# Layer 2's gate and value products over two units at once, 16-bit sums for norms, two raw loads from ScalarE, and a new table of shifts

## The chip, the cores and the metric

The kernel runs on one core of one Trainium2 chip. The metric is the device time of one execution in microseconds. A difference is told by the median of several runs.

## What is computed

Attention over 4 batches and 8 heads keeps, for each of 576 queries, the 32 largest scores. Its output, 2304 rows of 512, goes through two gated layers with an inner width of 1536. The weights arrive as 64-bit numbers, which the kernel converts itself; all other inputs have 32 bits.

```python
scores = scale * np.matmul(q, k.transpose(0, 1, 3, 2))
kth = np.partition(scores, -top_k, axis=-1)[..., -top_k:-top_k + 1]
scores = np.where(scores >= kth, scores, -1000000000.0)
attn = np.exp(scores - np.max(scores, axis=-1, keepdims=True))
attn = attn / (np.sum(attn, axis=-1, keepdims=True) + 1e-09)
x = np.matmul(attn, v)
...
xn = x / np.sqrt(np.mean(x * x, axis=-1, keepdims=True) + 1e-06) * rms_g
g = xn @ w_gate
x = (g / (1.0 + np.exp(-g)) * (xn @ w_val)) @ w_out
...
gate = 1.0 / (1.0 + np.exp(-(x @ w_gate2)))
out = (gate * (x @ w_val2)) @ w_out2
```

## The kernel before

**Units and tiles.** The 2304 rows form 18 units of 128 rows: four full ones for each batch of inputs, and one for each two batches that holds the 64 rows left over of both. For a unit, attention works through eight score tiles `sp` of 128 x 576 (144 in all). `attend` (line 721) makes one: TensorE writes the scores, VectorE finds the 32 largest by four MAX8 and three MATCH_REPLACE8, ScalarE takes the exponential `e`, VectorE masks it, ScalarE and GpSimd split it in two 16-bit parts `ph`, a DMA transposes them, and TensorE multiplies with v into `pv`. Two score banks rotate, so a score product waits until VectorE is done with the tile two before it.

**Precision.** Each 32-bit operand of a product is held as two 16-bit parts, and each product is three: high with high, high with low, low with high. `product` (line 862) writes 128 x 512 results from 48 such products (four blocks `m` of 128, four blocks of the contraction, three pairs), with the weights as the stationary operand and 128 columns of the unit's transposed rows moving. `out2` (line 1000) has the unit stationary and 512 columns of weights moving.

**Layers.** Layer 1 of a unit is `enter1` (norm and transpose), `gate1` for each of three slices `j` (products `pg` and `pw`, then tanh, scale and products on ScalarE and GpSimd, result `ht1`), and `out1` (product `py`, result `yt` in two 16-bit parts). Layer 2 is `gate2` for each slice (`pg` and `pw` from `yt`, result `ht2`) and `out2` (`po`). `gated` (line 884) holds what gate1 and gate2 share. Layer 1's weights stay in SBUF; those of layer 2, converted once and parked in DRAM, are read again for each batch by `load2` (line 980) into the seven buffers that raw weights use too. `BATCHES` (line 59) groups the units for layer 2: one, then eight pairs, then one. The two units of a pair share the loads, but each has its own products, its own scale `gsc` and its own `yt`.

**Sums for norms.** `scale_of` (line 680) and `out1` add a column over all partitions by a 32-bit product with `ones32`; `prep_piece` (line 500) spreads a column over the partitions by a 32-bit product `wmt` with the unit matrix.

**Raw weights.** `load_f32` (line 465) fetches a 128 x 512 block of 64-bit numbers. The first seven (`FIRST`) are issued by ScalarE, all others by SP. For layer 1's weights a block takes two VectorE instructions (`dec` and the joining one), one on ScalarE and one on GpSimd.

**The order.** Nothing is issued as it is written. `Scheduler.record` collects every operation with a priority, and `order` (line 260) simulates the engines with the costs of `cost` (line 224): it always takes the operation that can begin first, and among those the smallest priority. `SHIFTS` (line 64) adds a number, a tenth of it in microseconds, to the priority of each group of operations. `SLACK` says by how much an operation of TensorE counts as late after its producer (1 us, or 2.5 after SP's) when the scheduler looks for operations that are safe to take. The outcome is one fixed order for each engine and for the queue of SP; an instruction that must wait holds all behind it on its engine. Every row of the profile therefore carries the line that issues them, 385.

Of the kernel before, what the change touches and what calls it, by code (L numbers as in the profile page):

```python
# [46 lines left out]
SLACK = (1000.0, 2500.0)  # L47
# [13 lines left out]
FIRST = 7  # L61
# [82 lines left out]
class _Op:  # L144
    __slots__ = "eng calls cost lat prio deps users waits tiles start end idx new later base safe".split()
# [10 lines left out]
class Scheduler:  # L156
# [67 lines left out]
    def cost(self, eng, method, args, kw, writes, reads):  # L224
# [6 lines left out]
        if eng == "tensor":  # L231
            rate = 0.6 if method == "matmul" and kw["rhs"].shadow.dtype == F32 else 2.4
            return math.prod(out.shape[1:]) / rate + 2.7, 200
# [7 lines left out]
        if eng == "scalar":  # L241
            if method == "dma_start":
                return self.move(method, out, n)
            return n * 0.8333 + (51 if psum else 93) + 93 * (ptrs + ("accum_out" in kw)), 200
        if eng == "gpsimd":
            if method == "tensor_tensor":
                return (516 if n == 1 else n * (1.88 if mybir.dt.size(out.dtype) == 2 else 2.1) + 149), 100
# [12 lines left out]
    def order(self):  # L260
# [3 lines left out]
        for op in self.ops:  # L264
            op.users, op.waits, op.start, op.end, op.new, op.later, op.safe = [], len(op.deps), 0.0, None, [], [], 0.0
# [35 lines left out]
        def choose(reach):  # L301
            best = None
            for eng in self.ENGINES:
                pick = None
                for op in ready[eng]:
# [10 lines left out]
                    key = (max(0.0, max(at, op.safe if eng == "tensor" else 0.0) - now[eng] - PATIENCE), op.prio, op.idx)  # L316
# [7 lines left out]
        while len(out) < len(self.ops):  # L324
# [40 lines left out]
            for u in op.users:  # L365
                late = SLACK[op.eng == "sync"] if u.eng == "tensor" else 0.0
                u.start = max(u.start, op.end + OWN if u.eng == op.eng != "sync" and not op.calls[0][0].startswith("dma") else done)
                u.safe = max(u.safe, done + late)
# [20 lines left out]
def topk_attention_moe_kernel(  # L389
# [33 lines left out]
    ones32 = const.tile([P, P], F32, name="ones32")  # L423
# [715 lines left out]
```

## Time and profile before

| what | value |
| --- | --- |
| median of 3 runs | 1242.55 us (1242.1 to 1243.56) |
| the profiled execution, its own time | 1239.67 us |
| its span, first to last instruction | 1237.6 us |
| TensorE busy | 1120.6 us, 17020 products |
| VectorE busy | 994.3 us |
| ScalarE busy | 857.3 us |
| GpSimd busy | 844.0 us |

The profile is of one execution. A busy time is the union of an engine's instructions. Products overlap in the pipeline, so the length of one product's record says less than the distance from one start to the next, or than a block's share of the chain of work that ended last. An idle time of an engine is put down to the event that ended it. PE is TensorE, PEld its weight loads, DVE VectorE, ACT ScalarE, POOL GpSimd and SP the queue of SyncE.

### The profile page before, as it was taken

The page shows a single profiled execution, that of the slowest core. Times are in us where ns is not written, and L with a number is a line of the kernel's source. Part 1 is how long each engine was busy: PE and PEld are TensorE (multiplying, and loading weights), DVE is VectorE, ACT ScalarE, POOL GpSimd, SP SyncE. Part 2 cuts the span into 40 slices and gives each one's busy share as a digit, 9 for nine tenths or more (in the row PEclk, how much of TensorE's full clock was granted, in tenths as well). Part 3 has the DMA queues.
Part 4 walks back from the last instruction along what each step waited for, and adds up shares of the span by engine and source line. Part 5 has one row for each costly group of instructions (what it writes and reads, how often), then busy time and mean ns, then how long its engine had stood idle before and what let it go on. Part 6 is the DMA issues. An engine that isn't in the chain of part 4 may idle for free.

```text
span 1237.6 us, 41694 instructions
## 1 busy us (share of the span) xinstructions
PE 1120.6 (91%) x17020; PEld 963.3 (78%) x17020; DVE 994.3 (80%) x2571; ACT 857.3 (69%) x1536; POOL 844.0 (68%) x966
## 2 busy tenths in 40 slices
PE   2776374689998999999999999999999999999998
PEld 1433263689798789978996999699789969997976
DVE  5899999898796999999889899998759999970001
ACT  5999889887686577686966577578657666762522
POOL 5898899897676568685876667587657666762430
PEclk9989576699999999999999999999999999999999
DMA  9895797889968765779868586868766766854347
GB/s 281 280 264 157 238 265 221 205 258 235 211 152 187 180 147 137 137 178 189 187 144 192 115 191 136 210 132 191 179 114 139 181 153 122 193 121 136 138 122 262
DMA packets 323775, 225.27 MB, mean 182 GB/s; under 512 B 278400, under 2 KB 286592, under 8 KB 323584
## 3 DMA queue, kind: packets, MB, share of 16 engines
q1 hardware_dynamic: 322576, 218.95, 72.7%
q10 hardware_dynamic: 1008, 3.67, 0.8%
q8 instruction: 133, 2.18, 0.7%
q14 instruction: 58, 0.48, 0.1%
HBM read 147.06 MB, written 14.16 MB: 130 GB/s over the span
## 4 chain that ended last, share of the span: by engine, by line
PE 60%; DVE 15%; ACT 8%; DMA 5%; issue 5%; POOL 5%; SPq 1%; ACTq 0%; POOLq 0%; DVEq 0%
PE pg L385 17%; PE pw L385 16%; PE py L385 9%; PE po L385 9%; DVE m L385 5%; DVE w L385 5%; PE sp L385 4%; PE pv L385 3%; DVE e L385 2%; DMA kr<-in_k_dram 1%; POOL ph L385 1%; PE wlo L385 1%; ACT raw L385 1%; ACT e L385 1%; DMA pt<-ph 1%
## 5 line engine op out<-in xcount | busy, mean ns | idle before, releaser
L385 DVE MAX8 m<-w 128x8 f32<-128x576 f32 x432 | 314.5, 749 | 1.5
L385 PEld LDWEIGHTS <-wl 128*128 128x128 f16 x5184 | 293.1, 98 | 1.7 <-issue 0.7
L385 POOL TENSOR_TENSOR ph<-e,ph 128x64 f16<-128x64 f32 (+1 forms) x288 | 204.3, 733 | 79.3 <-ACT ph L385 76.9
L385 DVE MATCH_REPLACE8 w<-m,w 128x576 f32<-128x576 f32 x288 | 213.0, 743 | 0.0
L385 PEld LDWEIGHTS <-w1v 128*128 128x128 f16 (+1 forms) x2640 | 150.3, 98 | 24.1 <-POOL w1v L385 16.8
L385 POOL TENSOR_TENSOR sg<-sg,sv 128x512 f32<-128x512 f32 x105 | 133.7, 1274 | 48.0 <-ACT sv L385 45.1
L385 ACT ACTIVATE e<-sp,nb,sc 128x576 f32<-128x576 f32 x144 | 116.1, 827 | 66.6 <-POOL nb L385 47.2
L385 PE MATMUL pg<-xt,w1g 128*128 128x128 f16 x2592 | 154.4, 220 | 2.9 <-DVE ym L385 1.3
L385 PE MATMUL pg<-yt,wl 128*128 128x128 f16 x2592 | 155.4, 220 | 0.7 <-DVE p2t L385 0.7
L385 PEld LDWEIGHTS <-w1o 128*128 128x128 f16 (+1 forms) x2640 | 152.9, 100 | 3.8 <-issue 2.6
L385 POOL TENSOR_TENSOR ht<-sg,ht 128x512 f16<-128x512 f32 x105 | 121.7, 1160 | 47.7 <-ACT ht L385 45.3
L385 PE MATMUL pw<-xt,w1v 128*128 128x128 f16 x2592 | 153.5, 219 | 0.7 <-ACT sf L385 0.6
L385 PE MATMUL pw<-yt,wl 128*128 128x128 f16 x2592 | 153.6, 219 | 0.0
L385 PEld LDWEIGHTS <-w1g 128*128 128x128 f16 (+1 forms) x2624 | 149.7, 98 | 3.6 <-issue 3.1
L385 PE MATMUL py<-ht,w1o 128*128 128x128 f16 x2592 | 150.2, 221 | 0.5 <-POOL ht L385 0.5
L385 PE MATMUL po<-wl,ht 128*128 128x512 f16 x648 | 144.4, 379 | 0.0
L385 ACT ACTIVATE ph<-e 128x576 f16<-128x576 f32 x144 | 96.3, 677 | 64.9 <-DVE e L385 56.9
L385 DVE MAX8 m<-sp 128x8 f32<-128x576 f32 x144 | 106.9, 757 | 35.8 <-PE sp L385 33.3
L385 PE MATMUL sp<-kt,qt 128*128 128x512 f16 (+3 forms) x640 | 94.1, 298 | 37.0 <-DVE e L385 25.1
L385 DVE SCALAR_TENSOR_TENSOR e<-sp,m,e 128x576 f32<-128x576 f32 x144 | 115.1, 809 | 3.2 <-ACT e L385 1.2
L385 PEld LDWEIGHTS <-ht 128*128 128x128 f16 x648 | 61.7, 98 | 70.0
L385 PEld LDWEIGHTS <-qt 128*128 128x128 f16 (+1 forms) x640 | 49.1, 103 | 80.2 <-DVE e L385 18.8
(167 smaller groups left out, 1849.8 us busy)
## 6 DMA issues: line engine op xcount, KB each, us to landing
wl<-w2g SPq DMA_DIRECT2D x60, 512.0 KB, 4.8
wl<-w2v SPq DMA_DIRECT2D x60, 512.0 KB, 4.8
wl<-w2o SPq DMA_DIRECT2D x60, 512.0 KB, 5.2
raw<-in_moe_w_out_dram SPq DMA_DIRECT2D x24, 512.0 KB, 5.1
raw<-in_moe_w_val_dram SPq DMA_DIRECT2D x21, 512.0 KB, 5.2
raw<-in_moe_w_gate_dram SPq DMA_DIRECT2D x20, 512.0 KB, 4.5
qr<-in_q_dram SPq DMA_DIRECT2D x32, 128.0 KB, 3.5
kr<-in_k_dram SPq DMA_DIRECT2D x16, 256.0 KB, 3.5
```

The source lines that it names most:

```text
L385: getattr(eng, method)(*map(real, a), **{n: real(x) for n, x in k.items()})
```

## The change

`gate2` runs over a pair. `product` takes the number of blocks `M` itself; for a pair it is 2, and each product moves 256 columns, the two units side by side, so that one call makes half of a slice for both units. `out1` writes its result into a `yt` that holds both units of a batch, two of which rotate (`YT`). In `gated` layer 2's tanh is taken unit by unit, since each has its own scale. `out2` finds its operands in the new layout. The first and the last batch keep one unit and 128 columns.

The sums for norms and `wmt` become one 16-bit pass: `top` reads the upper half of each 32-bit number as bfloat16, of the column and of the unit matrix; `ones` is bfloat16.

`FIRST` goes from 7 to 2. `cost` gets other numbers for products, for raw blocks and for their sums. The slack behind a producer now delays an operation of TensorE in the simulation itself, and only from 250 us on; the choice of safe operations is gone. `SHIFTS` is new throughout: entries from -259 to 382 before, from -1796 to 2230 now.

```diff
 OWN = 130.0
-SLACK = (1000.0, 2500.0)
+SLACK = (1000.0, 2500.0, 250000.0)
...
 AHEAD = 8
-FIRST = 7
+FIRST = 2
+YT = 2
...
 SHIFTS = (
...
 )
...
             rate = 0.6 if method == "matmul" and kw["rhs"].shadow.dtype == F32 else 2.4
-            return math.prod(out.shape[1:]) / rate + 2.7, 200
+            return max(math.prod(out.shape[1:]) / rate + 2.5, 28 if out.shape[-1] > 1 else 200 if rate < 1 else 60), 200
         if eng == "vector":
...
                 return self.move(method, out, n)
-            return n * 0.8333 + (51 if psum else 93) + 93 * (ptrs + ("accum_out" in kw)), 200
+            words = any(x.tile.args[2].startswith("raw") for x in reads)
+            return n * 0.8333 + (51 if psum else 93) + (75 if words and psum else 35 if words else 0) + 93 * (ptrs + ("accum_out" in kw)), 200
         if eng == "gpsimd":
             if method == "tensor_tensor":
+                if any(x.tile.args[2].startswith("raw") for x in reads):
+                    return n * 2.1 + 180, 100
                 return (516 if n == 1 else n * (1.88 if mybir.dt.size(out.dtype) == 2 else 2.1) + 149), 100
...
                             at = max(at, dma - BACKLOG)
-                    key = (max(0.0, max(at, op.safe if eng == "tensor" else 0.0) - now[eng] - PATIENCE), op.prio, op.idx)
+                    key = (max(0.0, at - now[eng] - PATIENCE), op.prio, op.idx)
                     if pick is None or key < pick[0]:
...
             for u in op.users:
-                late = SLACK[op.eng == "sync"] if u.eng == "tensor" else 0.0
-                u.start = max(u.start, op.end + OWN if u.eng == op.eng != "sync" and not op.calls[0][0].startswith("dma") else done)
-                u.safe = max(u.safe, done + late)
+                late = SLACK[op.eng == "sync"] if u.eng == "tensor" and op.end > SLACK[2] else 0.0
+                u.start = max(u.start, op.end + OWN if u.eng == op.eng != "sync" and not op.calls[0][0].startswith("dma") else done + late)
             for u in op.users + op.later:
...
     const = pool("const", 1)
-    ones32 = const.tile([P, P], F32, name="ones32")
-    nc.vector.memset(ones32, 1.0)
+    ones = const.tile([P, P], BF16, name="ones")
+    nc.vector.memset(ones, 1.0)
     mhalf = const.tile([P, 1], F32, name="mhalf")
...
+    def top(x):
+
+        return x.bitcast(BF16).rearrange("p (f a) -> p f a", a=2)[:, :, 1]
+
     def pow2_scale(m, n, name, pl=None, out=None):
...
         t = ps_m.tile([P, P], F32, name="wmt", tag="mm", lane="wps")
-        nc.tensor.matmul(t, lhsT=m.to_broadcast([P, P]), rhs=eye, start=True, stop=True)
+        nc.tensor.matmul(t, lhsT=top(m).to_broadcast([P, P]), rhs=top(eye), start=True, stop=True)
         m = tiny.tile([P, 1], F32, name="wx")
...
         t = ps_m.tile([P, 1], F32, name="kvt", tag="mm", lane="kvt")
-        nc.tensor.matmul(t, lhsT=ones32, rhs=n, start=True, stop=True)
+        nc.tensor.matmul(t, lhsT=ones, rhs=top(n), start=True, stop=True)
         return pow2_scale(t, 1, "kv", out=(sc[0][:, p, a : a + 1], sc[1][:, p, a : a + 1]))
...
-    def product(ps, b, k, ws, rhss):
-
-        M = spread(b)[0]
+    def product(ps, M, k, ws, rhss):
+
         with E.group():
...
-    def gated(b, k, rhs, wg, wv, gsc, vsc, silu, name, bufs, last=False, behind=None, sq=None):
-
-
-
-        M, U = spread(b)
+    def gated(mu, k, rhs, wg, wv, gsc, vsc, silu, name, bufs, last=False, behind=None, sq=None):
+
+
+
+        M, U = mu
         pg = ps_m.tile([P, M, U, P], F32, name="pg", tag="mm", lane=name)
...
             E.after(behind)
-        product(pg, b, k, [wg], [rhs])
-        pg = flat(pg)
+        product(pg, M, k, [wg], [rhs])
         sg = mo.tile([P, 512], F32, name="sg", bufs=3, lane=name)
-        nc.scalar.activation(sg, pg, AF.Tanh, scale=gsc)
+        if silu:
+            pg = flat(pg)
+            nc.scalar.activation(sg, pg, AF.Tanh, scale=gsc)
+        else:
+            for x, a in enumerate(gsc):
+                nc.scalar.activation(sg.rearrange("p (m u r) -> p m u r", m=M, u=U)[:, :, x], pg[:, :, x], AF.Tanh, scale=a)
         ht = htp.tile([P, 2, M, U, P], F16, name=name, bufs=bufs)
...
             pw = pw()
-            product(pw, b, k, [wv], [rhs])
+            product(pw, M, k, [wv], [rhs])
             nc.vector.scalar_tensor_tensor(out=sg, in0=sg, scalar=1.0, in1=flat(pw), op0=ALU.add, op1=ALU.mult)
...
         pw = pw()
-        product(pw, b, k, [wv], [rhs])
+        product(pw, M, k, [wv], [rhs])
         sv = m1.tile([P, 512], F32, name="sv", tag="tmp", bufs=3, lane="sv" + name)
...
             t = ps_m.tile([P, 1], F32, name="yn", tag="mm", lane="yn")
-            nc.tensor.matmul(t, lhsT=ones32, rhs=n, start=True, stop=True)
+            nc.tensor.matmul(t, lhsT=ones, rhs=top(n), start=True, stop=True)
             m = tiny.tile([P, 1], F32, name="ym")
...
             ys[b] = pow2_scale(m, 1, "y")
-            yts[b] = []
         s, i = ys[b]
...
         product(
-            py, b, k, [lay1["o"][0][j] for j in range(NJ)],
+            py, M, k, [lay1["o"][0][j] for j in range(NJ)],
             [columns(b, [ht1[b, j, x] for x in range(U)]) for j in range(NJ)],
...
         nc.scalar.activation(f, flat(py), AF.Copy, scale=s)
-        yt = mo.tile([P, 2, M, U, P], F16, name="yt", bufs=2)
-        hi, lo = (flat(yt[:, a]) for a in range(2))
+        d, x = inside[b]
+        if x == 0:
+            yts[d] = mo.tile([P, 2, CPJ, 2, P], F16, name="yt", bufs=YT)
+            in2[d] = []
+        f = f.rearrange("p (c r) -> p c r", r=P)
+        hi, lo = (yts[d][:, a, :, x] for a in range(2))
         nc.scalar.activation(hi, f, AF.Copy)
         nc.gpsimd.tensor_tensor(out=lo, in0=f, in1=hi, op=ALU.subtract)
-        yts[b].append(yt)
-        if k < U - 1:
-            return
         a = tmul(i, ik, name="ya")
...
             nc.vector.tensor_scalar(gsc[:, j], lay2["g"][2][:, j].bitcast(F32), a, 0.5, op0=ALU.mult, op1=ALU.mult)
-        in2[b] = (columns(b, yts[b]), gsc, a)
+        in2[d].append((gsc, a))
...
-    def gate2(d, b, j, k):
+    def gate2(d, j, k):
         for n in "gv":
...
                 load2(d, n, j)
-        rhs, gsc, _ = in2[b]
+        U = len(batches[d])
+        rhs = lambda c, a: yts[d][:, a, c, 0:U]
         last = d == len(batches) - 1
-        ht2[b, j, k] = gated(
-            b, k, rhs, w2[d, "g", j], w2[d, "v", j], gsc[:, j : j + 1], state["c2"][0][:, j : j + 1], False, "ht2", 6, last,
+        ht2[d, j, k] = gated(
+            (CPJ // U, U), k, rhs, w2[d, "g", j], w2[d, "v", j], [g[:, j : j + 1] for g, _ in in2[d]], state["c2"][0][:, j : j + 1], False, "ht2", 6, last,
             state["c2"][0] if d == 0 else None
...
             w = w2[d, "o", j]
-            for b in batches[d]:
-                ht = columns(b, [ht2[b, j, k] for k in range(len(groups[b]))])
-                for x, u in enumerate(groups[b]):
+            U = len(batches[d])
+            ht = lambda c, a: ht2[d, j, c * U // CPJ][:, a, c % (CPJ // U)]
+            for x, b in enumerate(batches[d]):
+                for u in groups[b]:
                     if j == 0:
...
                                 n += 1
-        for b in batches[d]:
+        for x, b in enumerate(batches[d]):
             for u in groups[b]:
-                osc = tmul(in2[b][2], state["c2"][1], name="osc")
+                osc = tmul(in2[d][x][1], state["c2"][1], name="osc")
                 o = mo.tile([P, 512], F32, name="acc", tag="sg", bufs=3, lane="acc")
...
             groups.append([next(units) for _ in range(n)])
+    inside = {b: (d, x) for d, bs in enumerate(batches) for x, b in enumerate(bs)}
     halves = lambda b: range(len(groups[b]))
...
     ]
-    second = lambda d: [(5.4, gate2, (d, b, j, k)) for j in range(NJ) for b in batches[d] for k in halves(b)] + [
+    second = lambda d: [(5.4, gate2, (d, j, k)) for j in range(NJ) for k in range(len(batches[d]))] + [
         (7.8 * sum(len(groups[b]) for b in batches[d]), out2, (d,))
...
```

The new order shows first on ScalarE at the very start of the program. `raw` is a block of raw weights, `gr` the squared gain, `qr`, `kr` and `vr` are the first q, k and v, `kvn` their sums of squares. Before:

```order
L385 DMA raw_109<-in_moe_w_gate_dram 128x1024
L385 DMA raw_118<-in_moe_w_gate_dram 128x1024
L385 DMA raw_124<-in_moe_w_gate_dram 128x1024
L385 DMA raw_128<-in_moe_w_gate_dram 128x1024
L385 DMA raw_132<-in_moe_w_val_dram 128x1024
L385 DMA raw_134<-in_moe_w_val_dram 128x1024
L385 DMA raw_136<-in_moe_w_val_dram 128x1024
L385 ACT_TABLE_LOAD
L385 ACTIVATE raw_109<-raw_109 128x512
L385 ACTIVATE raw_118<-raw_118 128x512
L385 ACTIVATE gr_120<-gr_120 128x512
L385 ACTIVATE raw_124<-raw_124 128x512
```

And with the change:

```order
L392 DMA raw_109<-in_moe_w_gate_dram 128x1024
L392 DMA raw_118<-in_moe_w_gate_dram 128x1024
L392 ACT_TABLE_LOAD
L392 ACTIVATE raw_109<-raw_109 128x512
L392 ACTIVATE raw_118<-raw_118 128x512
L392 ACTIVATE gr_120<-gr_120 128x512
L392 ACTIVATE qn_77_148,qn_147<-qr_124 128x256
L392 ACTIVATE ks_161,kvn_162<-kr_126 128x576
L392 ACTIVATE qn_77_148<-qr_124,qs_159 128x4x2x64
L392 ACTIVATE vt_177,kvn_178<-vr_130 128x640
L392 ACTIVATE qr_124<-qr_124,qs_159 128x256
L392 ACTIVATE ks_161<-kr_126,kvs_180 128x9x64
```

Five issues are gone from the front, the table load stands behind two, and the squares of q, k and v stand ahead of all later raw blocks.

On VectorE, the last rows ahead of the first MAX of a score tile (`wps` and `wmt` are sums over a piece of weights). Before, with the rows of the second and third piece in front of it:

```order
L385 TENSOR_SCALAR dec_356<-raw_280 128x512
L385 SCALAR_TENSOR_TENSOR w1v_21_355<-raw_280,dec_356 128x512
L385 TENSOR_REDUCE wx_366<-wmt_362 128x1
L385 TENSOR_SCALAR wn_373<-wx_366,g_27_153 128x1
L385 TENSOR_SCALAR p2t_377<-wn_373 128x1
L385 TENSOR_SCALAR w1vs_379<-p2t_377 128x1
L385 TENSOR_SCALAR w1vi_384<-w1vs_379 128x1
L385 MAX m_85_418<-sp_401 128x8
```

With the change:

```order
L392 TENSOR_REDUCE wm_262<-wps_230 128x1
L392 SCALAR_TENSOR_TENSOR w1g_20_256<-raw_184,dec_257 128x512
L392 TENSOR_REDUCE wx_268<-wmt_266 128x1
L392 TENSOR_SCALAR wn_273<-wx_268,g_27_152 128x1
L392 TENSOR_SCALAR p2t_276<-wn_273 128x1
L392 TENSOR_SCALAR w1gs_278<-p2t_276 128x1
L392 TENSOR_SCALAR w1gi_285<-w1gs_278 128x1
L392 MAX m_85_312<-sp_280 128x8
```

The first MAX now follows the sums of the first piece `w1g` (`wn_273`, `w1gs`) instead of those of the second (`w1vs`), behind nine blocks of raw weights instead of thirteen.

On TensorE, a `yn` that is followed by a layer 2 gate product, in the middle of the program. Before:

```order
L385 LDWEIGHTS qt_12186
L385 MATMUL sp_12496<-kt_11417,qt_12186 128x64
L385 MATMUL yn_12503<-hn_12251,ones_0_107 128x1
L385 LDWEIGHTS wl_2908_11751
L385 MATMUL pg_12505<-yt_9976,wl_2908_11751 128x128
```

With the change:

```order
L392 LDWEIGHTS w1o_25_963
L392 MATMUL py_11469<-ht_2876_11368,w1o_25_963 128x128
L392 LDWEIGHTS ones_107
L392 MATMUL yn_11674<-hn_11438,ones_107 128x1
L392 LDWEIGHTS wl_2905_11025
L392 MATMUL pg_11676<-yt_9311,wl_2905_11025 128x256
```

`yn` has a weight load of its own now, as 16-bit products do, and the product behind it makes 256 columns from one load instead of 128.

## Rows read from the trace of the kernel before

**Rows 1.** The page, part 1: busy us (share of the span) and instructions.

```profile
PE 1120.6 (91%) x17020; PEld 963.3 (78%) x17020; DVE 994.3 (80%) x2571; ACT 857.3 (69%) x1536; POOL 844.0 (68%) x966
```

**Rows 2.** Busy time by stretches: from, to, length, engines, granted clock, DMA share, GB/s.

```profile
0.00:40.00 40.00, 15.05 (x80) 9.58 (x80) 22.76 (x61) 23.22 (x45) 26.26 (x32) 1.00 0.91 286
40.00:250.00 210.00, 134.68 (x1244) 90.89 (x1243) 199.95 (x541) 190.46 (x341) 187.16 (x206) 0.74 0.83 229
...
300.00:1105.00 805.00, 796.21 (x13104) 711.43 (x13101) 716.67 (x1813) 555.57 (x1000) 548.42 (x648) 1.00 0.74 162
300.00:1237.60 937.60, 924.89 (x14911) 818.61 (x14907) 727.34 (x1846) 602.85 (x1079) 588.92 (x683) 1.00 0.71 164
```

**Rows 3.** VectorE's waits, 40 to 250 us (9 rows): total, times, longest.

```profile
DVE p2t L385 <- PE kvt L385: 1.5, 2, 1.3
...
DVE ms L385 <- ACT junk L385: 0.3, 1, 0.3
```

**Rows 4.** TensorE's waits, 300 us to the end (9 rows).

```profile
PE sp L385 <- DVE qi L385: 2.0, 1, 2.0
PE sp L385 <- DVE e L385: 1.7, 3, 1.1
...
PE kvt L385 <- ACT vt L385: 0.2, 1, 0.2
```

**Rows 5.** The chain that ended last, from 1100 us: start, us, what.

```profile
1106.94 0.42 PE pv L385 x14
...
1153.78 5.36 PE pg L385 x96
...
1196.71 12.95 PE po L385 x60
```

**Rows 6.** Groups by form, whole span: count, busy us, mean ns, idle before.

```profile
L385 PEld LDWEIGHTS <-wl 128*128 128x128 f16 x5184 | 293.1, 98 | 1.7 <-issue 0.7 <-DMA wl<-w2g 0.2
...
L385 ACT ACTIVATE sg<-pg,gsc 128x512 f32<-128x512 f32 x54 | 36.7, 679 | 15.7 <-PE pg L385 15.6
...
L385 ACT ACTIVATE qr<-qr,qs 128x256 f32<-128x256 f32 x36 | 18.1, 502 | 0.4
```

**Rows 7.** Timeline of TensorE, two places: start, us, instructions, idle before.

```profile
340.95 2.85 PE L385 MATMUL pg<-yt,wl 128*128 128x128 f16 x48
...
465.39 0.36 PE L385 MATMUL yn<-hn,ones 128*128 128x1 f32 x2
465.61 2.84 PE L385 MATMUL pw<-yt,wl 128*128 128x128 f16 x48
```

**Rows 8.** Groups by form on TensorE, 300 us to the end.

```profile
L385 PE MATMUL kvt<-kvn,ones 128*128 128x1 f32 x44 | 7.1, 242 | 1.1 <-ACT ks L385 0.9 <-ACT vt L385 0.2
L385 PE MATMUL yn<-hn,ones 128*128 128x1 f32 x32 | 5.4, 239 | 0.0
```

**Rows 9.** Timeline of all engines, 0 to 45 us.

```profile
0.72 9.31 ACTq L385 DMA_DIRECT2D raw<-in_moe_w_gate_dram  x4
...
5.34 0.69 DVE L385 SCALAR_TENSOR_TENSOR w1v<-raw,dec 128x512 int32<-128x512 int32 x1
...
10.51 1.30 ACTq L385 DMA_DIRECT2D raw<-in_moe_w_val_dram  x3
...
13.14 1.20 ACT L385 ACTIVATE raw<-raw 128x512 int32<-128x512 uint32 x2
...
20.50 0.68 ACT L385 ACTIVATE ks<-kr 128x576 bf16<-128x576 f32 x1
...
26.56 1.97 SPq L385 DMA_TRANSPOSE kt<-ks  x1
...
38.47 0.77 DVE L385 MAX8 m<-sp 128x8 f32<-128x576 f32 x1 [2.24 <-PE sp L385]
```

**Rows 10.** VectorE's waits, 0 to 40 us (6 rows, 16.6 us).

```profile
DVE g L385 <- ACT gr L385: 6.0, 1, 6.0
```

**Rows 11.** The chain that ended last, its beginning.

```profile
2.24 8.25 DMA kr<-in_k_dram
```

More of the change, by code (lines that the diff above doesn't have):

```diff
@@ L144 @@
 class _Op:
-    __slots__ = "eng calls cost lat prio deps users waits tiles start end idx new later base safe".split()
+    __slots__ = "eng calls cost lat prio deps users waits tiles start end idx new later base".split()
 class _Engine:
@@ L264, in order @@
         for op in self.ops:
-            op.users, op.waits, op.start, op.end, op.new, op.later, op.safe = [], len(op.deps), 0.0, None, [], [], 0.0
+            op.users, op.waits, op.start, op.end, op.new, op.later = [], len(op.deps), 0.0, None, [], []
         for op in self.ops:
@@ L941, in gate1 @@
         ht1[b, j, k] = gated(
-            b, k, rhs, lay1["g"][0][j], lay1["v"][0][j], gsc[:, j : j + 1], vsc[:, j : j + 1], True, "ht1", 3,
+            spread(b), k, rhs, lay1["g"][0][j], lay1["v"][0][j], gsc[:, j : j + 1], vsc[:, j : j + 1], True, "ht1", 3,
             behind=vsc if groups[b][0] < 2 else None, sq=hsq[b][:, j * U + k : j * U + k + 1],
```

32 rows, old and new, of the table SHIFTS are left out of this document.

## The prediction, made before the changed kernel was run

> **What bounds the kernel now.** I read the page first, then the table by stretches, then the waits of each stretch, and last the order of single instructions at the places the edit touches. The page says that TensorE is busy for 91% of the span and VectorE for 80% [rows 1], which settles nothing: both are means over stretches with different limits. The table by stretches tells them apart [rows 2]. Between 40 and 250 us VectorE is busy for 199.95 of 210 us, TensorE for 134.68, at a mean granted clock of 0.74 (so partly at 1.2 GHz and partly at 2.4). From 300 us to the end TensorE is busy for 924.89 of 937.6 us at a clock of 1.00 (2.4 GHz), and VectorE for 727.34. So VectorE sets the pace until about 250 us, and TensorE from 300 us on.
>
> Two further views support that. In 40 to 250 us all that VectorE waited for adds up to about 9 us, none of it longer than 1.3 us [rows 3]. From 300 us to the end the listed waits of TensorE add up to 8.6 us in 937.6 [rows 4]. From 300 us on, the end is therefore the moment at which TensorE becomes full plus the work it still has. Two things can move it: less work per product behind 300 us, or an earlier moment. What the other engines do there is hidden as long as they keep up; VectorE had 88 us to spare between 300 and 1105 us (805 less its busy 716.67) [rows 2], and ScalarE is busy for 602.85 of 937.6 us.
>
> **The wide products.** The change takes two units through layer 2's gate and value products at once, in the eight batches that have two units. Of the 5184 products of 128 columns, 4608 become 2304 of 256; the first and the last batch have one unit and stay. The chain gives the step of a product at full clock [rows 5]: 96 of 128 columns in 5.36 us are 55.8 ns each, 60 of 512 columns in 12.95 us are 215.8 ns. A straight line through the two is 0.4167 ns a column and 2.5 ns for each product, so 256 columns should take 109.2 ns where two of 128 took 111.7. That is 2.5 ns x 2304 = 5.7 us, all of it behind 300 us on the full engine. Bounds: nothing, if the step of 256 columns carries more of its own; and, if the 2.5 ns vanished wholly, 111.7 - 106.7 = 5.0 ns each, 11.5 us. I take 5.7, the value on the line.
>
> Here a page speaks for much more. The Trainium skill (TensorE: Matmul & The Clock Gate, Back-to-back issue gap) gives a sustained spacing of load and product pairs of about 81 ns at 128 columns and 131 ns at 512. An estimate from that page, in between, is 98 ns at 256, which would save 2304 x (162 - 98) = 147 us. The trace disagrees: its steps are 55.8 and 215.8 ns, in proportion to the columns. So the weight load (98 ns in its records, one per product [rows 6]) is hidden behind the moving columns already, and removing 2304 of them frees a unit that was not the limit.
>
> **The 16-bit sums.** The sums over partitions for `kvt` and `yn` are products of one column that run as two passes of 32 bits. One took 0.22 us on the full engine, from 465.39 to the next product's start at 465.61 [rows 7]. Behind 300 us there are 32 records of `yn` and 44 of `kvt` [rows 8], two to a sum, so 38 sums. What one 16-bit pass with its load will take is not in the trace. The nearest rows are 30 ns for a step of 65 columns (14 in 0.42 us) [rows 5], and those 30 ns behind a load of 98 ns in the open [rows 6], 0.13 us. I take 0.07 us, nearer the first since loads mostly run ahead, so 0.15 us x 38 = 5.7 us; the ends are 3.4 and 7.2 us. The 18 products `wmt` fall too, but they belong to the preparation of the weights, ahead of the full stretch, where TensorE has a third of its time free [rows 2]: nothing.
>
> **The start.** ScalarE now issues two loads of raw weights instead of seven. In the kernel before, the first four issues took until 10.03 us, since they waited for landed loads, the last three went out only at 10.51, and ScalarE's first useful instruction came at 13.14 [rows 9]. Behind it stood the squares of k (20.50), and with them the transposed k (issued from 26.56 to 28.53); the first MAX8 of attention began at 38.47. VectorE was busy for 22.76 of these 40 us [rows 2] and waited for 16.6, of which 6.0 for ScalarE's `gr` [rows 10].
>
> Now the table load stands directly behind two issues. The first k had landed at 10.49 us (2.24 and 8.25) [rows 11], and its squares could begin there, 10 us sooner. From the squares to the end of the transpose's issue took 8.0 us; with the transpose's landing, v's squares ahead of it and the weight sum that TensorE's order still has in front, some 5 us together, the first MAX8 comes near 24 us. VectorE's order has nine raw tiles ahead of it instead of thirteen, at two instructions each of 0.69 us [rows 9], so by 24 us VectorE has done 9 x 1.38 us and some 4 us of small operations, 16.5 us, and idled for 7 or 8 instead of 16. Not all that is won lasts, since tiles must be ready to fill the time: I take 7 us off the moment at which TensorE becomes full, with ends at 0 and 12.
>
> The five loads that ScalarE no longer issues go to SP's queue, behind k and v of the first pair and ahead of the first transposes of q and k. The three that ScalarE issued last took 1.30 us [rows 9], so five take 2.2 us and their waits for landed predecessors, inside the 10 us by which k's squares move forward.
>
> **What costs nothing.** Layer 2's tanh over 512 columns becomes two over 256 in 48 blocks, because each unit has its own scale. From 679 ns at 512 columns, and 502 ns for 256 on ScalarE [rows 6], that is 0.33 us more in each, 16 us in all on an engine that is idle for a third of the stretch [rows 2]; the bank is released 0.3 us later, and three rotate. If ScalarE's slack were gone, those 16 us would be the price. Writing `yt` for two units side by side changes strides alone. Layer 2 of a pair must now wait for the second unit's `yt`; before, the first such product stood at 340.95 us [rows 7], where TensorE was full and had other work. Two wider buffers in place of two narrow ones let out1 run further ahead. I put these two against each other at nothing, with 3 us either way.
>
> **The sum.** The profiled execution took 1239.67 us with a span of 1237.6. Less 5.7, 5.7 and 7.0, that is 1221.3. The median of the three runs, 1242.55, stands 2.9 us above the profiled execution, so I forecast **1224 us**. The terms' ends alone give 1242.55 - 11.5 - 7.2 - 12 - 3 = 1209 at best and 1242.55 - 0 - 3.4 - 0 + 3 = 1242 at worst.
>
> **Rivals.** *The start gives nothing* (chance 0.19). For it: the DMA engines are busy 0.91 of the first 40 us at 286 GB/s [rows 2]; if attention's first tiles come sooner but the raw weights do not, VectorE waits later for the same bytes. Against it: its longest wait there was for ScalarE, not for a load [rows 10]. Then 1242.55 - 11.4 = 1231 us.
>
> *TensorE waits for VectorE* (chance 0.14, slower). The whole table of shifts is new, with entries of up to 223 us where 38 was the largest, and each engine keeps its written order: a score product whose bank VectorE has not released stops everything behind it on TensorE. Before, such waits behind 300 us came to 3.7 us [rows 4]. There are about 114 score tiles left there. Priced by the order's rows, the 120th tile stands behind 769 us of TensorE work instead of 800, some 10 us more than the shorter products explain, so VectorE has to be earlier there. From 0.18 us a tile (21 us) the gain is lost and the kernel slower; at 0.35 us a tile, 40 us, the time is 1242.55 - 18.4 + 40 = 1264 us. VectorE's 88 us of idle time speak against it. Waits of 16 to 21 us, which leave no change, have 0.06.
>
> *The order fills the early gaps* (chance 0.07): TensorE is idle for 75 of the 210 us from 40 to 250 [rows 2]; if ten of these carry layer products that stood behind 300, the time is 1214, and with the other good ends near 1206.
>
> *The weight load sets the step* (chance 0.01). The steps of rows 5, which grow 3.87 times with four times the columns at one load each, speak against it. If the load and not the columns did set the 55.8 ns, half of the loads would free 2304 x 55.8 ns = 129 us, and the time would be near 1110. [...]
>
> **How the numbers follow.** My forecast has 0.53, at 1214 to 1230. Faster by more than 0.2% (2.5 us, about what a measurement can tell from no change) is the sum of forecast, lost start, filled gaps and weight loads: 0.53 + 0.19 + 0.07 + 0.01 = 0.80. Same 0.06, slower 0.14. The range 1206 to 1242 takes in the bounds and the lost start, and leaves out the slower case and the far side of the gains.
>
> **What would show it.** In the changed profile: 1152 `pg<-yt` of 256 columns, 24 of them in about 2.62 us on the chain; a `yn` step below 0.1 us; ScalarE's table load before 3 us; the first MAX8 of scores before 28 us; TensorE at 49 of 50 us from some 290 us on with listed waits under 12 us. Wrong would be a first MAX8 still beyond 35 us, waits of `sp` for VectorE above 20 us behind 300, or a block of 24 that takes much less than 2.6 us.

## The result and the profile after

The changed kernel took 1223.05 us in the median of four runs (1220.78 to 1225.63) beside 1242.32 us for the kernel before: a ratio of 0.9846, with a 95% interval of 0.9822 to 0.9869. Taken again later (last experiment) it was 1220.84 us, a ratio of 0.9808 (0.9788 to 0.9829). The forecast was 1224 us. The profiled execution took 1220.78 us with a span of 1219.0; against before's 1237.6 that is 18.6 us less, where the sum of the terms said 18.4.

The page, part 1, of the changed kernel (it answers to [rows 1]):

```profile
PE 1098.5 (90%) x14648; PEld 915.3 (75%) x14648; DVE 993.8 (82%) x2571; ACT 862.4 (71%) x1584; POOL 844.9 (69%) x966
```

Its busy time by stretches, with the columns of [rows 2]:

```profile
0.00:40.00 40.00, 14.12 (x59) 7.40 (x60) 28.83 (x80) 27.37 (x51) 26.37 (x34) 0.97 0.94 291
40.00:250.00 210.00, 129.04 (x1240) 87.10 (x1239) 199.97 (x534) 189.53 (x341) 191.37 (x209) 0.78 0.84 233
250.00:300.00 50.00, 49.09 (x877) 46.98 (x875) 46.46 (x122) 40.02 (x73) 40.94 (x47) 1.00 1.05 266
300.00:1105.00 805.00, 796.06 (x11167) 683.23 (x11164) 711.45 (x1816) 565.74 (x1053) 556.60 (x654) 1.00 0.72 163
300.00:1219.00 919.00, 906.28 (x12484) 773.78 (x12480) 718.54 (x1837) 605.45 (x1123) 586.21 (x679) 1.00 0.69 164
```

VectorE gained 6.1 us of work in the first 40 us (28.83 for 22.76) and is as full as before until 250. TensorE is full from 250 us on (49.09 of 50; 45.94 before). From 300 us to the end it is idle for 12.7 us in both kernels and busy for 18.6 us less now (906.28 for 924.89).

The start in the timeline (start, us, instructions; beside [rows 9]), and VectorE's waits of the first 40 us (total, times, longest; beside [rows 10]):

```profile
0.72 0.91 ACTq L392 DMA_DIRECT2D raw<-in_moe_w_gate_dram  x2
...
1.66 1.28 ACT L392 ACT_TABLE_LOAD   x1 [1.66 <-PEq L1142]
...
9.59 0.68 ACT L392 ACTIVATE ks<-kr 128x576 bf16<-128x576 f32 x1 [0.72 <-DMA kr<-in_k_dram]
...
16.76 3.79 SPq L392 DMA_TRANSPOSE kt<-ks  x1
...
23.82 0.77 DVE L392 MAX8 m<-sp 128x8 f32<-128x576 f32 x1 [0.65 <-PE sp L392]
```

```profile
DVE dec L392 <- DMA raw<-in_moe_w_gate_dram: 5.4, 3, 3.7
DVE p2t L392 <- PE kvt L392: 3.7, 3, 2.4
DVE ones L392 <- PEq L1142: 0.8, 1, 0.8
DVE m L392 <- PE sp L392: 0.6, 1, 0.6
```

The table load follows two issues, the squares of k wait for their own load and no longer for ScalarE, and the first MAX8 comes 14.7 us sooner. VectorE's wait for `gr` is gone; 10.5 us of waits are left of 16.6. The lead over the kernel before does not last: counted by the first MAX8 of every score tile, it is 4.0 us at the 13th tile (154.9 for 158.9) and gone at the 25th (260.0 for 257.7); by the 31st it is 8.2 us (295.4 for 303.6). VectorE is as full in both from 40 to 250 us, so what moves the tiles there is the other work that each order puts between them.

Groups by form over the whole span, of the changed kernel (count, busy us, mean ns, idle before), beside [rows 6, 8]:

```profile
L392 PE MATMUL pg<-yt,wl 128*128 128x256 f16 x1152 | 133.6, 273 | 0.0
...
L392 PE MATMUL yn<-hn,ones 128*128 128x1 bf16 x18 | 3.0, 168 | 0.0
...
L392 PEld LDWEIGHTS <-wl 128*128 128x128 f16 x2880 | 254.4, 98 | 25.6
...
L392 ACT ACTIVATE sg<-pg,gsc 128x256 f32<-128x256 f32 x96 | 41.4, 465 | 3.9 <-PE pg L392 3.1 <-PE yn L392 0.7
```

TensorE's timeline in two places with a `yn` and the product behind it, beside [rows 7]:

```profile
557.30 0.17 PE L392 MATMUL yn<-hn,ones 128*128 128x1 bf16 x1
557.32 8.20 PE L392 MATMUL py<-ht,w1o 128*128 128x128 f16 x144
...
618.42 0.17 PE L392 MATMUL yn<-hn,ones 128*128 128x1 bf16 x1
618.45 2.78 PE L392 MATMUL pg<-yt,wl 128*128 128x256 f16 x24
```

The chain that ended last holds both widths, a pair's block of layer 2 and, behind it, one of layer 1 with 128 columns, `pg` from `xt` (beside [rows 5]):

```profile
1128.10 2.62 PE pw L392 x24
1130.72 2.68 PE pg L392 x48
```

A 16-bit sum lets the next product start after 0.02 to 0.03 us, where the 32-bit one took 0.22. A block of 24 products of 256 columns takes 2.62 us, one of 48 products of 128 takes 2.68. TensorE's waits from 300 us on, eight rows that add up to 8.4 us (8.6 before, [rows 4]), begin with:

```profile
PE sp L392 <- DVE e L392: 3.5, 4, 1.7
PE sp L392 <- DVE p2t L392: 1.9, 1, 1.9
```

### The profile page after: what moved, and what is told of

The parts are those of the page before. It is cut to its first block, busy times and chain, and to the rows that moved or that the text cites. A ratio compares the mean times of both kernels' runs of the same rounds, so it can differ in the third digit from the quotient of the medians.

```text
span 1219.0 us, 36897 instructions
## 1 busy us (share of the span) xinstructions
PE 1098.5 (90%) x14648; PEld 915.3 (75%) x14648; DVE 993.8 (82%) x2571; ACT 862.4 (71%) x1584; POOL 844.9 (69%) x966
## 4 chain that ended last, share of the span: by engine, by line
PE 51%; DVE 9%; POOL 8%; ACT 6%; issue 4%; DMA 2%; SPq 0%; POOLq 0%; ACTq 0%; DVEq 0%
PE pg L392 15%; PE pw L392 15%; PE po L392 7%; PE py L392 7%; DVE m L392 4%; DVE w L392 4%; PE sp L392 3%; PE pv L392 3%; POOL sg L392 2%; POOL ph L392 2%; POOL ht L392 2%; ACT sg L392 1%; ACT e L392 1%; DVE e L392 1%; DMA vr<-in_v_dram 1%
## 5 line engine op out<-in xcount | busy, mean ns | idle before, releaser
L392 PEld LDWEIGHTS <-wl 128*128 128x128 f16 x2880 | 254.4, 98 | 25.6
L392 POOL TENSOR_TENSOR ph<-e,ph 128x512 f16<-128x512 f32 (+1 forms) x288 | 205.6, 736 | 88.2 <-ACT ph L392 79.8
L392 PE MATMUL pg<-xt,w1g 128*128 128x128 f16 x2592 | 157.7, 222 | 1.9 <-DMA xt<-sn 1.9
L392 PEld LDWEIGHTS <-w1g 128*128 128x128 f16 (+1 forms) x2624 | 153.0, 99 | 3.9 <-issue 2.6
L392 PEld LDWEIGHTS <-w1o 128*128 128x128 f16 (+1 forms) x2640 | 150.4, 99 | 2.0 <-issue 0.7
L392 PE MATMUL pw<-yt,wl 128*128 128x256 f16 (+1 forms) x1440 | 150.7, 262 | 0.1
L392 PE MATMUL pg<-yt,wl 128*128 128x256 f16 (+1 forms) x1440 | 150.7, 262 | 0.0
L392 ACT ACTIVATE ht<-sg 128x512 f16<-128x512 f32 x105 | 65.9, 627 | 68.0 <-POOL sg L392 67.9
```

Source lines behind the costliest of these rows:

```text
L392: getattr(eng, method)(*map(real, a), **{n: real(x) for n, x in k.items()})
```

## The experiments

Two theories stood at first: that the gain is the sum of the three parts as forecast (5.7, 5.7 and 7.0 us), and that much of it is the new order, for which the forecast had no term. In the first six kernels every engine keeps the order of the kernel that is named; only the part in question is changed. Times are compared by their ratios to the kernel before. A ratio is known to some 0.002 either way, and the changed kernel's own two ratios lie 0.0038 (4.7 us) apart, so a distance from their mean holds to 3 or 4 us either way.

### The changed kernel without one of its parts

*Narrow products*: layer 2's products of 256 columns become two of 128 from the same weights.

```diff
-        product(pg, M, k, [wg], [rhs])
+        (product if silu else product2)(pg, M, k, [wg], [rhs])
...
+                for x in range(U):
...
+                                    rhs=rhs(c, a)[:, x],
```

> The changed kernel with each product of 256 columns of a pair split again into two of 128, one unit after the other, and with the changed kernel's order of everything kept. Theory (TensorE is full behind 300 us and each product costs 2.5 ns of its own): 2304 products more, so 5.8 us slower than the changed kernel, ratio to the kernel before about 0.989; blocks of 48 in 2.68 us where 24 took 2.62. Rival (the new order brings the gain, the shorter products vanish in waits): under 2 us slower.

Measured: 1230.85 us, ratio to before 0.9892 (0.9869 to 0.9915). The mean of the changed kernel's two ratios is 0.9827, so the narrow products cost 0.0065, 8 us. Its chain shows blocks of 48 in 2.68 us in the pairs too. The step of the forecast is right; the time is a little over it, and inside its ends (0 to 11.5). In the profiled executions TensorE is busy for 6.0 us more from 300 us to the end (912.28 for 906.28; the row is counted to 1300 us, beyond the end):

```profile
300.00:1300.00 1000.00, 912.28 (x14780) 806.12 (x14775) 718.87 (x1837) 606.85 (x1122) 586.87 (x680) 1.00 0.65 151
```

*32-bit sums*: `ones`, `kvt`, `yn` and `wmt` as before.

```diff
-    ones = const.tile([P, P], BF16, name="ones")
+    ones = const.tile([P, P], F32, name="ones")
...
-        nc.tensor.matmul(t, lhsT=ones, rhs=top(n), start=True, stop=True)
+        nc.tensor.matmul(t, lhsT=ones, rhs=n, start=True, stop=True)
```

> The changed kernel with the sums for norms and wmt in 32 bits again, order kept. Theory: 38 sums behind 300 us cost 0.15 us more each, so 5.6 us slower than the changed kernel, ratio about 0.989; wmt, ahead of the full stretch, adds nothing. Rival (sums are hidden like wmt): under 1 us. Second rival (the chain from sum to scale to layer products matters more than the product's own time): over 9 us, with more waits of TensorE for VectorE's scale.

Measured: 1225.28 us, ratio 0.9853 (0.9829 to 0.9877), 0.0026 or 3 us above the changed kernel. The same two places of TensorE's timeline in this kernel:

```profile
559.07 0.36 PE L392 MATMUL yn<-hn,ones 128*128 128x1 f32 x2
559.29 8.20 PE L392 MATMUL py<-ht,w1o 128*128 128x128 f16 x144
...
620.65 0.33 PE L392 MATMUL yn<-hn,ones 128*128 128x1 f32 x2
620.84 2.78 PE L392 MATMUL pg<-yt,wl 128*128 128x256 f16 x24
```

Each sum takes 0.16 to 0.20 us more, a little over the forecast's 0.15. The 3 us, with 3.6 either way, are not clear of nothing, nor of the 5.6 expected. In the two profiled executions the account closes: TensorE is busy for 7.2 us more from 300 us on (913.51 for 906.28), its listed waits fall to 5.7 us from 8.4, and the span is 4.6 us longer (1223.6). There, part of what a sum takes is time in which TensorE would have waited anyway.

```profile
300.00:1300.00 1000.00, 913.51 (x12542) 781.73 (x12539) 720.22 (x1839) 607.22 (x1126) 587.68 (x680) 1.00 0.65 152
```

*Seven loads from ScalarE*: five of the issues go back behind ScalarE's first two.

```diff
+        if 2 <= state["raws"] < 7:
+            E.moved.append(E.ops[-1])
...
+            for op in self.moved:
+                op.eng = "scalar"
+            for op in ops[:at] + self.moved + ops[at:]:
```

> The changed kernel with the first seven raw loads on ScalarE again, put ahead of its table load, order otherwise kept. Theory of the prediction (a blocked ScalarE delays the start, and the start moves the moment at which TensorE is full): 5 to 7 us slower than the changed kernel, first MAX8 of scores beyond 30 us. Rival (the 14.7 us of head start at the first tile are lost by the 24th anyway, and the order alone decides how much layer work is done before 300 us): first MAX8 late all the same, but under 2 us slower in the end. Second rival (with this order, which relies on the early start, the whole delay is kept): 10 us or more.

Measured: 1227.37 us, ratio 0.9872 (0.9851 to 0.9893), 0.0045 or 5.6 us above. The start of this kernel in the timeline:

```profile
10.72 1.30 ACTq L397 DMA_DIRECT2D raw<-in_moe_w_val_dram  x3
12.05 1.28 ACT L397 ACT_TABLE_LOAD   x1 [12.05 <-issue]
...
15.37 0.67 ACT L397 ACTIVATE ks<-kr 128x576 bf16<-128x576 f32 x1
...
28.33 0.76 DVE L397 MAX8 m<-sp 128x8 f32<-128x576 f32 x1
```

The table load is 10.4 us later and the first MAX8 only 4.5 (it was expected beyond 30 us). Of the 14.7 us by which the start moved, the loads alone thus bring 4.5 in this order; the rest comes with the order (it has the squares of k ahead of the later raw blocks). The 4.5 us last: at the 31st score tile, when TensorE has become full, this kernel is still 4.3 us behind the changed one. First the changed kernel's row, then this one's:

```profile
295.39 0.75 DVE L392 MAX8 m<-sp 128x8 f32<-128x576 f32 x1
299.67 0.75 DVE L397 MAX8 m<-sp 128x8 f32<-128x576 f32 x1
```

That is the path which the prediction named: a later start, and TensorE full as much later.

*All three undone*, the edits above together, in the changed kernel's order:

> The changed kernel with all three undone, narrow products, 32-bit sums and seven loads on ScalarE, in the changed kernel's order. Theory: the three add, 5.8 + 5.6 + 5 to 7, so some 17 us slower than the changed kernel and within 3 us of the kernel before (ratio 0.998 to 1.002): the order by itself brings next to nothing. Rival (the order brings the gain): still 8 us or more faster than the kernel before.

Measured: 1234.03 us, ratio 0.9924 (0.9904 to 0.9944). The parts together are worth 0.0097, 12 us (3 either way). One by one they cost 17, but that difference is within the noise: the profiled executions give 16.7 one by one and 15.3 together. Some 9 us of the gain, 7 to 12 by the interval, remain when all three are gone, and the forecast had no term for those. Where they lie no trace shows: the profiled execution was the slowest of its six (1236.08 us), with a span only 3.3 us below that of the kernel before (1234.3 for 1237.6). The order reaches into the start as well: the first MAX8 still comes at 29.08 us here, 9.4 sooner than before, though that lead is gone by the 13th tile (159.5 for 158.9).

### The kernel before with one part

*Two loads from ScalarE*: five issues move to SP, behind the first k and v.

```diff
+            for op in self.moved:
+                op.eng = "sync"
+            for op in head + self.moved + [op for op in ops if op not in head]:
```

> The kernel before with five of ScalarE's seven raw loads moved to SP, behind the first k and v, all else in the order of before. Theory (the blocked ScalarE costs the start): ScalarE begins near 5 us instead of 13, but in the old order the squares of k still stand behind all seven raw tiles, so the first MAX8 comes 3 to 8 us sooner and the kernel is 2 to 5 us faster (ratio 0.996 to 0.998). Rival (loads alone do nothing without the new order): first MAX8 and time unchanged within 1.5 us.

Measured: 1238.24 us, ratio 0.9958 (0.9946 to 0.997): 5.2 us gained, just over what the theory said. Here ScalarE's table load stands at 1.65 us, but its order still has seven raw blocks ahead of the squares of k (two in the changed kernel), and the first MAX8 comes at 34.66, 3.8 us sooner.

*16-bit sums:*

```diff
-        nc.tensor.matmul(t, lhsT=ones32, rhs=n, start=True, stop=True)
+        nc.tensor.matmul(t, lhsT=ones32, rhs=top(n), start=True, stop=True)
```

> The kernel before with the sums for norms and wmt in one 16-bit pass, order of before kept. Theory: 38 sums behind 300 us at 0.15 us, 5.6 us faster (ratio 0.9955), the same size as undoing them in the changed kernel. Rival (a shorter sum on TensorE is eaten by waits that the old order has elsewhere): under 2 us faster.

Measured: 1239.91 us, ratio 0.9976 (0.9964 to 0.9988): 3.0 us gained, and 4.5 at most by the interval. That is between theory and rival, and less than the 5.6 expected. TensorE's listed waits from 300 us on rise from 8.6 to 12.0 us in the profiled execution, which would be the same exchange as above, seen from the other side; but it is not shown. That execution was the slowest of twelve (1243.2 us) and late long before TensorE was full: its first MAX8 stands at 40.61 us and its 31st score tile begins at 309.3, where the kernel before has 38.47 and 303.6. Where the rest of the 5.6 us went stays open.

### The orders without their shifts

The table of shifts is set to zero in either kernel, and the planner's own rule makes the order.

```diff
-SHIFTS = (
...
-)
+SHIFTS = (0,) * 1000
```

> The changed kernel with every entry of the table of shifts set to 0, so that the scheduler orders by the plain priorities. Theory (TensorE is full behind 300 us in either order, shifts only pack it): listed waits of TensorE behind 300 us grow from 8 us to 20 to 60 us and the kernel is that much slower than the changed one, ratio to before 1.00 to 1.04. Rival (the table matters little): within 5 us of the changed kernel.

> The kernel before with every entry of its table of shifts set to 0. Theory: as for the changed kernel without shifts, 20 to 60 us slower than before (ratio 1.015 to 1.05). The distance to the changed kernel without shifts tells what the change is worth without a table made for it: the theory says 10 to 20 us, a rival that the gain hangs on the table says under 5.

Measured: 1251.25 us (ratio 1.0057, 1.0039 to 1.0076) with the change and 1251.3 us (1.0058, 1.004 to 1.0077) without it. The whole change without its table is worth nothing, to some 3 us either way. The new table brings about 29 us, the old one 7, where 20 to 60 were expected of either. In the stretches of the changed kernel with zero shifts, VectorE, which sets the pace there, is busy 9.7 us less from 40 to 250 us than with the table, and TensorE 14.5 us less from 300 to 1105:

```profile
40.00:250.00 210.00, 127.15 (x1207) 86.07 (x1206) 190.30 (x505) 184.08 (x332) 185.56 (x200) 0.76 0.83 231
...
300.00:1105.00 805.00, 781.59 (x10944) 671.78 (x10942) 710.33 (x1801) 559.13 (x1031) 541.92 (x641) 0.99 0.72 162
```

VectorE's listed waits from 40 to 250 us are 18.0 us here, 14.6 in the kernel before with zero shifts, and 7.7 and 9.1 with the tables. TensorE's from 300 to 1105 are 22.7 us here; no row is long:

```profile
PE sp L373 <- DVE e L373: 4.2, 5, 1.6
PE pv L373 <- DVE sc L373: 2.7, 1, 2.7
PE kvt L373 <- ACT vt L373: 2.6, 1, 2.6
```

From 300 us to the end the two kernels without shifts compare as follows, with the change first:

```profile
300.00:1300.00 1000.00, 921.50 (x12627) 785.95 (x12624) 732.44 (x1859) 616.10 (x1132) 592.00 (x687) 0.99 0.65 154
300.00:1300.00 1000.00, 929.96 (x14987) 822.94 (x14983) 739.00 (x1864) 609.89 (x1087) 593.70 (x690) 1.00 0.66 155
```

With the change TensorE is busy for 8.5 us less there, but idle for 27.2 us to the end of the span at 1248.7, instead of 18.8 to 1248.8. What it saved is lost as idle time.

That left open why the change, with 12 us less in its parts, gains nothing without a table. Theory A: work taken off TensorE becomes waits in an order that was not made for it. Theory B: the parts keep their worth, and what else changed (the common `yt`, the planner's costs and slack) makes a worse order by as much.

*All three parts undone*, by the same edits, in the order of the changed kernel with zero shifts:

> The changed kernel with all shifts at zero, and its wide products, 16-bit sums and two loads undone; every engine keeps the order that the kernel with zero shifts had (only the five issues go back to ScalarE). It took 1251 us with the three parts in. Theory A (work taken off TensorE turns into waits in an order that was not made for it): the parts are worth at most 5 us in this order, so 1251 to 1256 us, and TensorE's listed waits from 300 to 1105 us, 22.7 us with the parts in, shrink to 12 to 18. Theory B (each part is worth what its work says, in any order, and the order with zero shifts was merely unlucky by as much): 11 us or more slower, 1262 to 1267 us, with waits still above 20 us.

Measured: 1263.85 us, ratio 1.0148 (1.0122 to 1.0175), 0.0091 or 11 us above. Theory B is nearer: the parts are worth 11 us here (4 either way) and 12 us with the table. Theory A, at most 5 us, falls as the main account, though TensorE's waits did shrink a little, from 22.7 to 19.4 us (it had said 12 to 18, theory B above 20). The layout and the new planner without shifts cost 0.0090 against the old planner without shifts (1.0148 and 1.0058), 11 us (4 either way), and that just eats up the parts. This order was planned with the parts in, though, and no run tells how much of the 11 us comes of running it without them.

*The slack set to zero*, all shifts zero:

```diff
-SLACK = (1000.0, 2500.0, 250000.0)
+SLACK = (0.0, 0.0, 250000.0)
```

> The changed kernel with all shifts at zero and with the slack behind a producer set to zero, so that the planner chooses without it. Theory A (the new rule on slack spoils an order without shifts, and the table has to mend it): 1238 to 1245 us, with TensorE's listed waits from 300 to 1105 us at 8 to 15 us instead of 22.7. Theory B (the slack is not what costs; without it TensorE is put still closer behind its producers): 1250 to 1262 us, with waits of 22 us or more.

Measured: 1261.25 us, ratio 1.0118 (1.0084 to 1.0153), 0.0061 or 8 us slower than with the slack. So the slack helps, and the loss sits elsewhere; theory B holds, with listed waits of 29.9 us from 300 to 1105 us. The first row of TensorE's waits from 300 us to the end shows what the slack is for:

```profile
PE pv L373 <- DMA pt<-ph: 21.7, 14, 3.3
```

Planned close behind its transpose, `pv` holds up all of TensorE until the transpose lands; with the slack, this row has 1.5 us. Two stretches, the kernel without slack first in each pair, show that more than the waits was lost:

```profile
300.00:400.00 100.00, 87.66 (x1294) 76.72 (x1292) 76.31 (x205) 67.90 (x130) 64.07 (x74) 0.92 0.79 173
300.00:400.00 100.00, 92.65 (x1386) 82.10 (x1384) 79.04 (x214) 72.69 (x138) 66.98 (x77) 0.97 0.83 185
...
300.00:1300.00 1000.00, 926.85 (x12627) 789.50 (x12624) 738.21 (x1856) 612.47 (x1131) 590.97 (x685) 0.99 0.66 153
300.00:1300.00 1000.00, 921.50 (x12627) 785.95 (x12624) 732.44 (x1859) 616.10 (x1132) 592.00 (x687) 0.99 0.65 154
```

The same 12627 products keep TensorE busy for 5.4 us longer. From 300 to 400 us, where it idles for 12.3 us instead of 7.3, its granted clock is 0.92 instead of 0.97 (1.00 in the changed kernel with its table, idle there for 4.4), so part of that stretch ran at 1.2 GHz. Which of the common `yt`, the two wide buffers, the cost numbers and the rule of safe operations that was dropped makes the order without shifts 11 us longer was not tried apart.

### The changed kernel again

> The changed kernel once more, unaltered, beside the two above, for a closer median to set the earlier experiments against: both theories expect 1221 to 1226 us, and TensorE's listed waits from 300 us to the end between 5 and 11 us (8.4 in the first profile).

Measured: 1220.84 us (1220.58 to 1221.09), ratio 0.9808 (0.9788 to 0.9829), with listed waits of TensorE from 300 us on of 7.5 us. The changed kernel's worth in the experiments is the mean of this ratio and the first.

## Why the prediction was right, and where its terms were not

**The bound** stood as told: VectorE until 250 us, then TensorE with waits under 9 us. All that the forecast named as signs is there: 1152 `pg<-yt` of 256 columns, 24 in 2.62 us, a step of `yn` under 0.1 us, the table load at 1.66 us, the first MAX8 at 23.82, TensorE at 49 of 50 us (from 250 on, sooner than the 290 named).

**The wide products**: 5.7 us were forecast; putting the narrow ones back costs 8 us, with an interval of some 4 us either way, and 6.0 us of TensorE's busy time. The line through the steps of [rows 5] gave 109.2 ns, and 2.62 us over 24 is 109.2 ns. An estimate from the spacings that the Trainium skill gives for pairs of load and product (TensorE: Matmul & The Clock Gate, Back-to-back issue gap: about 81 ns at 128 columns, 131 ns at 512) would have freed far more, and is not borne out here: 2304 loads went (5184 to 2880), and the step still follows the columns.

**The 16-bit sums** were priced too high. A sum saves 0.16 to 0.20 us, and there are 38 of them behind 300 us (22 `kvt` and 16 `yn`), so 6 to 7.6 us of TensorE's time, at the upper end of the forecast; but they are worth 3 us of the kernel's time in both directions tried (3.6 either way in the changed kernel, 1.5 in the kernel before, which alone rules the 5.7 out). The step that fell short is the one that let every microsecond on a full engine count. In the changed kernel's profiles 2.7 us of it are waits; in the kernel before the cause is open.

**The start** was forecast at 7 us, its first MAX8 at 24. The time of the MAX8 was met, and the forecast had counted the order's part of it too: loads and order together. The loads alone account for 4.5 us of the shift and for 5 to 6 us of the total, and those 4.5 last until TensorE is full; of the order's 9.4 us nothing is left at the 13th tile.

**What was put at nothing.** Layer 2's tanh costs 2 x 465 - 679 = 251 ns more in each of 48 blocks, 12 us where 16 were estimated, and is hidden: from 300 us on TensorE's listed waits for ScalarE come to 2.2 us, before 2.1. ScalarE is busy there for 605.45 us, before 602.85. The layout was put at nothing with 3 us either way, and the new table had no term at all, only two rivals. Together they brought about 9 us with the table; the layout and the new planner cost some 11 without it. That is the step which failed most. That the total came within 4 us of 1224 is in part luck: the three parts together gave 12 us instead of 18.4, and what had no term gave 9, two errors of opposite sign.

**The rivals.** That TensorE waits for VectorE was right as a danger: with zero shifts TensorE waits for 22.7 us, for VectorE, ScalarE, GpSimd and transposes alike, and the time is 1251 us; with the table the waits are 8.4. The start giving nothing is refuted by both runs on the loads. That the order fills the early gaps holds in part. Priced at their steps (columns x 0.4167 + 2.5 ns, the line through [rows 5]; without the one-column sums), the products that TensorE still has ahead at 300 us come to 906.2 us, before 917.4. Of these 11.2 us less the wide products explain 5.8; some 5 are work that was brought forward (7 in the second profile, 904.4), where the rival had ten. With the 6 to 7.6 us of the sums, that accounts for the 18.6 us of busy time.

## What to carry to other kernels

Time taken off the engine that sets the end need not count in full: 6 us and more of shorter sums gave 3 here. Look at the waits that come back, and price the order itself, by running old and new with the order's tuning taken out. The parts of this change are worth 12 us, and the whole of it nothing without a table made for it; what is not in the parts brought nearly as much as they did. At the start, five issues ahead of ScalarE's first work delayed its table load by 10.4 us and the first score tile by 4.5, and that was worth 5 to 6 us at the end.

## What was not expected of the hardware

A one-column 16-bit sum with its own weight load holds TensorE for 0.02 to 0.03 us between its neighbours, although its record is 168 ns: the forecast had taken 0.07. In the kernel without slack, `pt` took 3.2 us from issue to landing at the least, 3.8 in the median and 8.4 at the most between 300 and 1105 us, and products planned close behind one waited for up to 3.3 us:

```profile
DMA to landing us min/median/max: 3.2/3.8/8.4
```
